# One matrix in place of two, and a new way for the routing data: a clustered attention and FFN kernel on one core

## The chip, the cores and the metric

The kernel runs on one core of a Trainium2 chip. The metric is device time in microseconds (us) of one execution of the program. TensorE is called PE here, VectorE DVE, ScalarE ACT, GpSimd POOL and SyncE SP, as the profile calls them; PEld is TensorE's loading of stationary operands. "DMA share" is the mean busy share of the core's 16 DMA engines, which by the profile's count can come out slightly above 1, "clock" the granted TensorE clock as a fraction of full speed.

A single core has no second core beside it to tell a disturbed run by. A run is called slow when it is over 1.5% above the fastest run of the same kernel. The times quoted for the experiments are medians of all runs, slow ones included; the ratios use fast runs alone.

## The reference, cut to what matters

There are 4 batches of 8 heads, 768 tokens and 64 dimensions. Every query and key is assigned to one of 16 clusters of its head, and attention is limited to pairs of the same cluster. The 3072 resulting rows of 512 go through a feed-forward network (FFN) whose only non-linearity is the product of two projections.

```python
q_assign = argmax(einsum(q_n, c_n));  k_assign = argmax(einsum(k_n, c_n))   # 16 clusters
mask   = q_assign[:, :, :, None] == k_assign[:, :, None, :]
scores = where(mask, scale * q @ k.T, -1e9)
attn   = softmax(scores) @ v                        # (4, 8, 768, 64)
x = attn.transpose(0, 2, 1, 3).reshape(3072, 512)
a = x @ w1                                          # (3072, 1024)
b = x @ w2
h = a * b @ w3                                      # w3 is (1024, 1024)
return h @ w_out                                    # w_out is (1024, 512)
```

Nothing stands between `@ w3` and `@ w_out`, so the two matrices can be multiplied beforehand.

## The kernel before

Each head passes four stages: load, prep, route, and scores with exp; the product with v follows one head later. Prep splits q and k into a bf16 part and a bf16 rest, side by side, and lets a transposing DMA turn them. ACT and DVE do the casts:

```python
stg = bstage.tile([P, 2, NCH, P], BF16, name="stg")
nc.scalar.copy(out=stg[:, 0, :, 0:D], in_=q32)
nc.vector.tensor_tensor(out=stg[:, 0, :, D:P], in0=q32, in1=stg[:, 0, :, 0:D], op=ALU.subtract)
# ... the same for k; v is cast on DVE ...
nc.sync.dma_start_transpose(out=xqk, in_=stg)
```

Route scores the clusters, builds a one-hot row per token, transposes it and writes it under the operand, in rows 64 to 79, so that the score matmul adds the mask by itself. It does so for q and for k, with six narrow transposes each:

```python
for which, sign in ((0, -1), (1, 1)):
    xt = xqk[:, which, :, :]
    prr = psum_f.tile([P, NCH, C, 2], F32, name="prr", tag="f")
    # ... six matmuls into prr; rsc = sum of its pairs; mx = maximum ...
    nc.vector.tensor_tensor(out=oh, in0=rsc, in1=mx..., op=ALU.is_ge)
    pso = psum_f.tile([P, NCH, P], BF16, name="pso", tag="f")
    for j in range(NCH):
        nc.tensor.transpose(out=pso[0:C, j, :], in_=oh[:, j, :], identity=ident)
    # ... DVE scales pso into xt[64 : 64 + C] ...
```

A score tile spans two PSUM banks (2 x 384 columns), and one exp reads it. The FFN of a batch runs in two blocks of 384 tokens, in units between the heads of the next batch (five units a head):

```python
def make_h(kc):                      # the product with w3
    def unit():
        ph = psum_f.tile([P, SH], F32, name="ph", tag="f")
        for jc in range(8):
            nc.tensor.matmul(ph, lhsT=w3b[:, jc, kc * P : (kc + 1) * P], rhs=abs_[:, jc, :],
                             start=(jc == 0), stop=(jc == 7))
        # ... hsb[:, kc] = ph, on ACT or DVE ...
def make_out(sub):                   # the product with w_out
    # ... po += hsb[:, kc, 128 tokens].T @ wob[:, kc]  for kc in 0..7 ...
```

The weights come as f32 through one staging buffer, each chunk cast on DVE, two chunks a head during the first 12 heads:

```python
ws = wstage.tile([P, DFF], F32, name="ws", tag="ws")      # the pool has one buffer
nc.scalar.dma_start(ws[:, 0:ncols], wsrc[:, cc, :])
nc.vector.tensor_copy(out=wdst[:, cc, :], in_=ws[:, 0:ncols])
```

The softmax here doesn't subtract the row's maximum and nothing guards it: scores larger than these inputs give would overflow.

Of the kernel before, what the change touches and what calls it, by code (L numbers as in the profile page):

```python
# [18 lines left out]
SH = 384  # L19
DFF = 1024  # L20
DM = 512
NTOK = B * S
MASKB = 256.0
SM_SCALE = 0.125
VCOL = D + 1
NG = B * H
FFN_UNITS_PER_HEAD = 5
# [3 lines left out]
def kernel(  # L31
# [12 lines left out]
    nc = tc.nc  # L44

    const = ctx.enter_context(tc.tile_pool(name="const", bufs=1))
    wstage = ctx.enter_context(tc.tile_pool(name="wstage", bufs=1))
    setup = ctx.enter_context(tc.tile_pool(name="setup", bufs=2))

    fstage = ctx.enter_context(tc.tile_pool(name="fstage", bufs=6))  # L50
    bstage = ctx.enter_context(tc.tile_pool(name="bstage", bufs=4))
    xtp = ctx.enter_context(tc.tile_pool(name="xtp", bufs=5))
    rtp = ctx.enter_context(tc.tile_pool(name="rtp", bufs=3))
    expp = ctx.enter_context(tc.tile_pool(name="expp", bufs=12))
    rcpp = ctx.enter_context(tc.tile_pool(name="rcpp", bufs=3))
    xtmp = ctx.enter_context(tc.tile_pool(name="xtmp", bufs=2))
    ffnp = ctx.enter_context(tc.tile_pool(name="ffnp", bufs=2))
    outp = ctx.enter_context(tc.tile_pool(name="outp", bufs=2))

    psum_sc = ctx.enter_context(tc.tile_pool(name="psum_sc", bufs=2, space=bass.MemoryType.PSUM))  # L60
    psum_av = ctx.enter_context(tc.tile_pool(name="psum_av", bufs=2, space=bass.MemoryType.PSUM))
    psum_f = ctx.enter_context(tc.tile_pool(name="psum_f", bufs=2, space=bass.MemoryType.PSUM))

    ident = const.tile([P, P], BF16, name="ident")
    make_identity(nc, ident)

    xT_all = const.tile([P, 4, NTOK], BF16, name="xT_all")

    cen = setup.tile([P, D], F32, name="cen")
    nc.sync.dma_start(cen, centroids.rearrange("h c d -> (h c) d"))  # L70
# [27 lines left out]
    cnt2 = const.tile([P, H, C, 2], BF16, name="cnt2")  # L98
    for which in range(2):
        pct = psum_f.tile([P, P], BF16, name="pct", tag="f")  # L100
        nc.tensor.transpose(out=pct, in_=cnsrc[:, which, :], identity=ident)
        nc.vector.tensor_copy(
            out=cnt2[:, :, :, which],
            in_=pct[:, :].rearrange("p (h c) -> p h c", c=C),
        )

    w1b = const.tile([P, 4, DFF], BF16, name="w1b")
    w2b = const.tile([P, 4, DFF], BF16, name="w2b")
    w3b = const.tile([P, 8, DFF], BF16, name="w3b")
    wob = const.tile([P, 8, DM], BF16, name="wob")  # L110

    wsrcs = []
    for wsrc, wdst, nchunks, ncols in (
        (moe_w1.rearrange("(fc p) j -> p fc j", p=P), w1b, 4, DFF),
        (moe_w2.rearrange("(fc p) j -> p fc j", p=P), w2b, 4, DFF),
        (moe_w3.rearrange("(jc p) kk -> p jc kk", p=P), w3b, 8, DFF),
        (moe_w_out.rearrange("(kc p) m -> p kc m", p=P), wob, 8, DM),
    ):
        for cc in range(nchunks):
            wsrcs.append((wsrc, wdst, cc, ncols))  # L120
    wcast_pending = list(wsrcs)

    def emit_weight_casts(n):
        for _ in range(n):
            if not wcast_pending:
                return
            wsrc, wdst, cc, ncols = wcast_pending.pop(0)
            ws = wstage.tile([P, DFF], F32, name="ws", tag="ws")
            nc.scalar.dma_start(ws[:, 0:ncols], wsrc[:, cc, :])
            nc.vector.tensor_copy(out=wdst[:, cc, :], in_=ws[:, 0:ncols])  # L130

    def block_units(t0: int):
        st = {}

        def make_ab(jc):
            def unit():
                if "asb" not in st:
                    st["asb"] = ffnp.tile([P, 8, SH], BF16, name="asb")
                    st["abs_"] = ffnp.tile([P, 8, SH], BF16, name="abs_")
                asb = st["asb"]  # L140
                abs_ = st["abs_"]
                pa = psum_f.tile([P, SH], F32, name="pa", tag="f")
                for fcc in range(4):
                    nc.tensor.matmul(  # L144
                        pa,
                        lhsT=w1b[:, fcc, jc * P : (jc + 1) * P],
                        rhs=xT_all[:, fcc, t0 : t0 + SH],
                        start=(fcc == 0),
                        stop=(fcc == 3),
                    )  # L150
                nc.scalar.copy(out=asb[:, jc, :], in_=pa)  # L151
                pb = psum_f.tile([P, SH], F32, name="pb", tag="f")
                for fcc in range(4):
                    nc.tensor.matmul(  # L154
                        pb,
                        lhsT=w2b[:, fcc, jc * P : (jc + 1) * P],
                        rhs=xT_all[:, fcc, t0 : t0 + SH],
                        start=(fcc == 0),
                        stop=(fcc == 3),
                    )  # L160
                nc.vector.tensor_tensor(out=abs_[:, jc, :], in0=pb, in1=asb[:, jc, :], op=ALU.mult)  # L161

            return unit

        def make_h(kc):
            def unit():
                if "hsb" not in st:
                    st["hsb"] = ffnp.tile([P, 8, SH], BF16, name="hsb")
                hsb = st["hsb"]
                abs_ = st["abs_"]  # L170
                ph = psum_f.tile([P, SH], F32, name="ph", tag="f")
                for jc in range(8):
                    nc.tensor.matmul(  # L173
                        ph,
                        lhsT=w3b[:, jc, kc * P : (kc + 1) * P],
                        rhs=abs_[:, jc, :],
                        start=(jc == 0),
                        stop=(jc == 7),
                    )
                if kc % 2 == 0:  # L180
                    nc.scalar.copy(out=hsb[:, kc, :], in_=ph)  # L181
                else:
                    nc.vector.tensor_copy(out=hsb[:, kc, :], in_=ph)  # L183

            return unit

        def make_out(sub):
            def unit():
                hsb = st["hsb"]
                po = psum_f.tile([P, 512], F32, name="po", tag="f")  # L190
                for kc in range(8):
                    nc.tensor.matmul(  # L192
                        po,
                        lhsT=hsb[:, kc, sub * P : (sub + 1) * P],
                        rhs=wob[:, kc, :],
                        start=(kc == 0),
                        stop=(kc == 7),
                    )
                osb = outp.tile([P, DM], F32, name="osb")
                nc.vector.tensor_copy(out=osb, in_=po)  # L200
                bb = t0 // S
                sb = (t0 % S) // P + sub
                out_perm = out.rearrange("(bb pp six) m -> bb six pp m", pp=P, six=NCH)
                nc.sync.dma_start(out_perm[bb, sb], osb)

            return unit

        units = [make_ab(jc) for jc in range(8)]
        units += [make_h(kc) for kc in range(8)]
        units += [make_out(sub) for sub in range(3)]  # L210
        return units

    def ffn_units(b: int):
        return block_units(b * S) + block_units(b * S + SH)

    state = {}

    def stage_load(g: int):
        b, h = g // H, g % H
        st = state.setdefault(g, {})  # L220
        q32 = fstage.tile([P, NCH, D], F32, name="q32")
        nc.sync.dma_start(q32, q[b, h].rearrange("(p j) d -> p j d", p=P))
        k32 = fstage.tile([P, NCH, D], F32, name="k32")
        nc.sync.dma_start(k32, k[b, h].rearrange("(p j) d -> p j d", p=P))
        v32 = fstage.tile([P, NCH, D], F32, name="v32")
        nc.sync.dma_start(v32, v[b, h].rearrange("(p j) d -> p j d", p=P))
        st["q32"], st["k32"], st["v32"] = q32, k32, v32

    def stage_prep(g: int):
        st = state[g]  # L230
        q32, k32, v32 = st["q32"], st["k32"], st["v32"]
        stg = bstage.tile([P, 2, NCH, P], BF16, name="stg")
        nc.scalar.copy(out=stg[:, 0, :, 0:D], in_=q32)
        nc.vector.tensor_tensor(
            out=stg[:, 0, :, D:P], in0=q32, in1=stg[:, 0, :, 0:D], op=ALU.subtract
        )
        nc.scalar.copy(out=stg[:, 1, :, 0:D], in_=k32)
        nc.vector.tensor_tensor(
            out=stg[:, 1, :, D:P], in0=k32, in1=stg[:, 1, :, 0:D], op=ALU.subtract
        )  # L240
        vb = xtp.tile([P, NCH, 72], BF16, name="vb")
        nc.vector.tensor_copy(out=vb[:, :, 0:D], in_=v32)
        nc.vector.memset(vb[:, :, D:VCOL], 1.0)
        xqk = xtp.tile([P, 2, NCH, P], BF16, name="xqk")
        nc.sync.dma_start_transpose(out=xqk, in_=stg)
        st["vb"], st["xqk"] = vb, xqk
# [110 lines left out]
    for i in range(5):  # L357
        stage_load(i)
# [57 lines left out]
```

## Time and profile before

The median of three runs was 491.62 us (488.81 to 492.89). I cut the profiled execution, 495 us long, into six stages. The start lasts until the first score matmul. Each batch's attention ends where its tokens are ready for the FFN. The tail is the rest. Batch 0 has no FFN of an earlier batch beside it; the tail has no attention.

| stage | length, us | what runs in it |
|---|---|---|
| start | 26.0 | loads, prep, first route |
| batch 0 | 99.0 | attention alone, weights arriving |
| batch 1 | 110.4 | attention + FFN of batch 0 |
| batch 2 | 104.8 | attention + FFN of batch 1 |
| batch 3 | 93.5 | attention + FFN of batch 2 |
| tail | 61.4 | FFN of batch 3 |

The first view is the page of the kernel before: the engine table (busy us, share of the span, instructions), then three rows of the strip of 40 slices. Each digit is the share in tenths: PE's busy share, its granted clock, the DMA share.

```profile
...
PE 398.6 (81%) x3514; PEld 237.7 (48%) x3522; DVE 238.3 (48%) x675; ACT 221.6 (45%) x355; POOL 0.7 (0%) x6
...
PE   0279555772877899997987999998999999699996
...
PEclk9999955565889899999799999999999999979999
DMA  8997989688878254237432332126111000310101
...
```

PE is busy in most of the span, but from the second to about the eighth slice the clock digits fall to 5 and PE's own digits are 5 to 8. The windows view of the same kernel, with one line for each stage, gives this in numbers. Its columns are named in its first line.

```profile
...
core 0: us, PE busy (x) PEld busy (x) DVE busy (x) ACT busy (x) POOL busy (x), PEclk, DMA share, GB/s
0.00:26.00 26.00, 3.08 (x32) 1.97 (x32) 14.72 (x52) 8.48 (x15) 0.70 (x6) 1.00 1.02 262
26.00:125.00 99.00, 62.73 (x615) 38.73 (x616) 47.00 (x144) 46.80 (x67) 0.00 (x0) 0.69 0.88 170
125.00:235.40 110.40, 96.45 (x878) 57.46 (x881) 63.07 (x177) 59.12 (x99) 0.00 (x0) 0.95 0.56 141
235.40:340.20 104.80, 94.45 (x879) 56.72 (x882) 54.58 (x156) 53.63 (x86) 0.00 (x0) 0.98 0.31 68
340.20:433.70 93.50, 85.30 (x811) 52.60 (x813) 41.42 (x116) 42.07 (x65) 0.00 (x0) 0.99 0.18 39
433.70:495.10 61.40, 56.55 (x302) 30.22 (x304) 17.54 (x30) 11.50 (x24) 0.00 (x0) 0.96 0.10 32
...
```

In batch 0 PE is busy for 62.7 us of 99, at a mean clock of 0.69, with a DMA share of 0.88. In batches 1 to 3 and the tail it is busy for 87 to 92%, at 0.95 to 0.99. The first part waits; the rest is bound by PE. The waits view of before names the waits (total us, times, longest us):

```profile
...
PE pso L276 <- DVE oh L268: 23.4, 16, 9.4
...
DVE w3b L130 <- DMA ws<-in_moe_w_dram: 19.2, 4, 6.5
...
PE prr L256 <- DMA xqk<-stg: 11.6, 2, 6.4
...
DVE w2b L130 <- DMA ws<-in_moe_w_dram: 8.4, 1, 8.4
...
```

A cast that waits for a weight chunk (19.2 and 8.4 us in two of the lines) holds the routing that follows it on DVE, and PE then waits for the one-hots (`oh`, 23.4 us). The three groups of the page that the change touches (busy us, mean ns of one, idle time before):

```profile
...
L312 ACT ACTIVATE ex<-sc 128x768 bf16<-128x768 f32 x192 | 147.6, 810 | 79.0 <-PE sc L304 58.2
L304 PE MATMUL sc<-xqk 80*128 80x384 bf16 x384 | 104.4, 362 | 15.9 <-ACT ex L312 11.5
...
L276 PE MATMUL pso<-ident,oh 128*16 128x128 bf16 x384 | 37.1, 241 | 23.9 <-DVE oh L268 23.4
...
```

The page's chain of waits, followed back from the last instruction, gives PE 54% of the span and the DMAs 23%, and names the product with w3 (`ph`) as the largest single part:

```profile
...
PE 54%; DMA 23%; DVE 10%; ACT 7%; issue 3%; SPq 2%; ACTq 0%; DVEq 0%
PE ph L173 13%; DMA xqk<-stg 11%; PE sc L304 9%; PE po L192 8%; PE pb L154 8%; PE pa L144 6%; DMA ws<-in_moe_w_dram 6%; PE pso L276 5%; ACT ex L312 5%; DMA xT_all<-xtm 2%; PE av L324 2%; DMA ws<-in_moe_w_out_dram 2%; PE prr L256 2%; SPq L35
...
```

### The profile page before, as it was taken

The page shows a single profiled execution, that of the slowest core. Times are in us where ns is not written, and L with a number is a line of the kernel's source. Part 1 is how long each engine was busy: PE and PEld are TensorE (multiplying, and loading weights), DVE is VectorE, ACT ScalarE, POOL GpSimd, SP SyncE. Part 2 cuts the span into 40 slices and gives each one's busy share as a digit, 9 for nine tenths or more (in the row PEclk, how much of TensorE's full clock was granted, in tenths as well). Part 3 has the DMA queues.
Part 4 walks back from the last instruction along what each step waited for, and adds up shares of the span by engine and source line. Part 5 has one row for each costly group of instructions (what it writes and reads, how often), then busy time and mean ns, then how long its engine had stood idle before and what let it go on. Part 6 is the DMA issues. An engine that isn't in the chain of part 4 may idle for free.

```text
span 495.1 us, 8793 instructions
## 1 busy us (share of the span) xinstructions
PE 398.6 (81%) x3514; PEld 237.7 (48%) x3522; DVE 238.3 (48%) x675; ACT 221.6 (45%) x355; POOL 0.7 (0%) x6
## 2 busy tenths in 40 slices
PE   0279555772877899997987999998999999699996
PEld 0146333441544456554554555555655666345453
DVE  5555454442486465545344655554545554222322
ACT  4157443433563456555533465546444645122120
POOL 0000000000000000000000000000000000000000
PEclk9999955565889899999799999999999999979999
DMA  8997989688878254237432332126111000310101
GB/s 290 233 320 195 88 194 92 188 104 192 229 193 218 84 129 102 74 77 163 107 49 49 71 89 50 33 75 119 33 33 47 19 1 1 97 32 1 64 1 64
DMA packets 84152, 51.98 MB, mean 105 GB/s; under 512 B 65680, under 2 KB 77968, under 8 KB 84112
## 3 DMA queue, kind: packets, MB, share of 16 engines
q1 hardware_dynamic: 80656, 40.94, 37.8%
q10 hardware_dynamic: 3456, 10.49, 8.3%
q8 instruction: 27, 0.44, 0.4%
q14 instruction: 13, 0.11, 0.1%
HBM read 29.39 MB, written 6.29 MB: 72 GB/s over the span
## 4 chain that ended last, share of the span: by engine, by line
PE 54%; DMA 23%; DVE 10%; ACT 7%; issue 3%; SPq 2%; ACTq 0%; DVEq 0%
PE ph L173 13%; DMA xqk<-stg 11%; PE sc L304 9%; PE po L192 8%; PE pb L154 8%; PE pa L144 6%; DMA ws<-in_moe_w_dram 6%; PE pso L276 5%; ACT ex L312 5%; DMA xT_all<-xtm 2%; PE av L324 2%; DMA ws<-in_moe_w_out_dram 2%; PE prr L256 2%; SPq L352 2%; DVE rsc L264 1%
## 5 line engine op out<-in xcount | busy, mean ns | idle before, releaser
L312 ACT ACTIVATE ex<-sc 128x768 bf16<-128x768 f32 x192 | 147.6, 810 | 79.0 <-PE sc L304 58.2
L304 PE MATMUL sc<-xqk 80*128 80x384 bf16 x384 | 104.4, 362 | 15.9 <-ACT ex L312 11.5
L173 PEld LDWEIGHTS <-w3b 128*128 128x128 bf16 x512 | 50.2, 99 | 41.0 <-issue 9.0
L324 PEld LDWEIGHTS <-ex 128*128 128x128 bf16 x1152 | 56.5, 103 | 27.6 <-issue 8.2
L144 PE MATMUL pa<-xT_all,w1b 128*128 128x384 bf16 x256 | 56.0, 344 | 16.9 <-DMA xT_all<-xtm 14.5
L151 ACT CAST asb<-pa 128x384 bf16<-128x384 f32 x64 | 30.6, 478 | 84.8 <-PE pa L144 84.8
L324 PE MATMUL av<-vb,ex 128*128 128x65 bf16 x1152 | 63.4, 202 | 5.4 <-DVE xtm L333 3.7
L154 PE MATMUL pb<-xT_all,w2b 128*128 128x384 bf16 x256 | 55.5, 341 | 1.4 <-DVE abs__1460 L161 0.3
L276 PE MATMUL pso<-ident,oh 128*16 128x128 bf16 x384 | 37.1, 241 | 23.9 <-DVE oh L268 23.4
L304 PEld LDWEIGHTS <-xqk 80*128 80x128 bf16 x384 | 31.8, 102 | 28.7 <-issue 16.3
L276 PEld LDWEIGHTS <-oh 128*16 128x16 bf16 x384 | 23.7, 97 | 40.2 <-DVE oh L268 34.6
L144 PEld LDWEIGHTS <-w1b 128*128 128x128 bf16 x256 | 24.8, 101 | 37.3 <-issue 17.3
L192 PE MATMUL po<-wob,hsb 128*128 128x512 bf16 x184 | 41.8, 379 | 0.4
L183 DVE CAST hsb<-ph 128x384 bf16<-128x384 f32 x32 | 17.8, 557 | 47.7 <-PE ph L173 47.7
L181 ACT CAST hsb<-ph 128x384 bf16<-128x384 f32 x32 | 15.3, 479 | 54.2 <-PE ph L173 54.2
L154 PEld LDWEIGHTS <-w2b 128*128 128x128 bf16 x256 | 25.5, 101 | 24.2 <-issue 9.6
L256 PE MATMUL prr<-cnt_141,xqk 128*128 128x32 bf16 x384 | 20.4, 181 | 11.6 <-DMA xqk<-stg 11.6
L192 PEld LDWEIGHTS <-hsb 128*128 128x128 bf16 x192 | 18.8, 98 | 21.7
L200 DVE COPY osb<-po 128x512 f32<-128x512 f32 x24 | 16.6, 691 | 21.7 <-PE po L192 21.7
L264 DVE TENSOR_REDUCE rsc<-prr 128x96 f32<-128x192 f32 x64 | 22.7, 354 | 8.9 <-PE prr L256 7.8
L278 DVE TENSOR_SCALAR xqk<-pso 16x768 bf16<-16x768 bf16 x32 | 17.6, 549 | 19.4 <-PE pso L276 18.9
L256 PEld LDWEIGHTS <-xqk 128*128 128x128 bf16 x384 | 16.7, 99 | 20.9 <-DMA xqk<-stg 11.9
(214 smaller groups left out, 310.8 us busy)
## 6 DMA issues: line engine op xcount, KB each, us to landing
ws<-in_moe_w_dram ACTq DMA_DIRECT2D x16, 512.0 KB, 4.1
out_dram<-osb SPq DMA_DIRECT2D x24, 256.0 KB, 2.0
ws<-in_moe_w_out_dram ACTq DMA_DIRECT2D x8, 256.0 KB, 3.1
xqk<-stg SPq DMA_TRANSPOSE x32, 4.6
xT_all<-xtm SPq DMA_TRANSPOSE x24, 2.5
q_152<-in_q_dram SPq DMA_DIRECT2D x1, 192.0 KB, 3.8
k_154<-in_k_dram SPq DMA_DIRECT2D x1, 192.0 KB, 3.8
v_156<-in_v_dram SPq DMA_DIRECT2D x1, 192.0 KB, 3.9
```

Source lines behind the costliest of these rows:

```text
L144: nc.tensor.matmul(pa, lhsT=w1b[:, fcc, jc * P : (jc + 1) * P], rhs=xT_all[:, fcc, t0 : t0 + SH], start=(fcc == 0), stop=(fcc == 3),)
L151: nc.scalar.copy(out=asb[:, jc, :], in_=pa)
L154: nc.tensor.matmul(pb, lhsT=w2b[:, fcc, jc * P : (jc + 1) * P], rhs=xT_all[:, fcc, t0 : t0 + SH], start=(fcc == 0), stop=(fcc == 3),)
L173: nc.tensor.matmul(ph, lhsT=w3b[:, jc, kc * P : (kc + 1) * P], rhs=abs_[:, jc, :], start=(jc == 0), stop=(jc == 7),)
L183: nc.vector.tensor_copy(out=hsb[:, kc, :], in_=ph)
L192: nc.tensor.matmul(po, lhsT=hsb[:, kc, sub * P : (sub + 1) * P], rhs=wob[:, kc, :], start=(kc == 0), stop=(kc == 7),)
L256: nc.tensor.matmul(prr[:, j, :, :], lhsT=xt[:, j, :], rhs=cnt2[:, h, :, :], start=True, stop=True,)
L264: nc.vector.tensor_reduce(out=rsc, in_=prr, axis=AX.X, op=ALU.add)
L276: nc.tensor.transpose(out=pso[0:C, j, :], in_=oh[:, j, :], identity=ident)
L304: nc.tensor.matmul(sc[:, sh, 0:SH], lhsT=xk[0:80, j, :], rhs=xq[0:80, 3 * sh : 3 * sh + 3, :], start=True, stop=True,)
L312: nc.scalar.activation(out=ex, in_=sc[:, :, 0:SH], func=ACT.Exp, scale=SM_SCALE)
L324: nc.tensor.matmul(av[:, sub, 0:VCOL], lhsT=exs[j][:, sh, sub * P : (sub + 1) * P], rhs=vb[:, j, 0:VCOL], start=(j == 0), stop=(j == NCH - 1),
```

## The change

Its intent is fourfold. The product `w3 @ w_out` is formed once on the chip, in units between the heads of batch 0, so the FFN has two steps instead of three. One-hots are built for q and k together and transposed four chunks at once (3 transposes in place of 12), and four small DMAs put them in place. The casts of q, k, v and the weights leave ACT and DVE (those inside the FFN stay): GpSimd casts q, k and v, and the weight loads, issued by GpSimd, cast on the way. Score tiles take one bank (512 columns, or 2 x 256), with three buffers. Besides, each pair of heads is transposed for the FFN on PE (`psx`) instead of by a DMA at the end of a batch, and the FFN works in blocks of 512 tokens. The core of the diff:

```diff
-            ws = wstage.tile([P, DFF], F32, name="ws", tag="ws")
-            nc.scalar.dma_start(ws[:, 0:ncols], wsrc[:, cc, :])
-            nc.vector.tensor_copy(out=wdst[:, cc, :], in_=ws[:, 0:ncols])
+            nc.gpsimd.dma_start(dst, src)            # f32 to bf16 on the way
 ...
+        def make_t(kc):                              # w3 transposed, 8 units
+            pt = psum_f.tile([P, 8, P], BF16, name="pt", tag="f")
+            for jc in range(8):
+                nc.tensor.transpose(out=pt[:, jc], in_=w3b[:, jc, kc * P : (kc + 1) * P], identity=ident)
+            nc.vector.tensor_copy(out=w3T[:, kc], in_=pt...)
+        def make_w(jc):                              # wc = w3 @ w_out, 8 units
+            pw = psum_f.tile([P, DM], F32, name="pw", tag="f")
+            for kc in range(8):
+                nc.tensor.matmul(pw, lhsT=w3T[:, kc, jc * P : (jc + 1) * P], rhs=wob[:, kc], ...)
+            nc.vector.tensor_copy(out=wc[:, jc], in_=pw)
 ...
-        def make_h(kc):  ...  (ph and hsb are gone)
-                        lhsT=hsb[:, kc, sub * P : (sub + 1) * P], rhs=wob[:, kc, :],
+                        po, lhsT=st["ab"][:, jc, sub * P : (sub + 1) * P], rhs=wc[:, jc],
 ...  prep
-        nc.scalar.copy(out=stg[:, 0, :, 0:D], in_=q32)
-        nc.vector.tensor_tensor(out=stg[:, 0, :, D:P], in0=q32, ..., op=ALU.subtract)   # and for k
+        nc.gpsimd.tensor_copy(out=stg[:, :, 0:D], in_=qk32)
+        nc.gpsimd.tensor_tensor(out=stg[:, :, D:P], in0=qk32, in1=stg[:, :, 0:D], op=ALU.subtract)
+        nc.gpsimd.tensor_copy(out=vb[:, :, 0:D], in_=x32[:, 2])
 ...  route
-            for j in range(NCH):                     # for q and for k
-                nc.tensor.transpose(out=pso[0:C, j, :], in_=oh[:, j, :], identity=ident)
+        for r in range(3):
+            nc.tensor.transpose(out=pso[:, r], in_=oh[:, r].rearrange("p a c -> p (a c)"), identity=ident)
+        nc.vector.tensor_scalar(out=ohT, in0=pso, scalar1=msc[:, 0:1], scalar2=msc[:, 1:2], ...)
+        for a in range(4):
+            nc.sync.dma_start(xqk[D : D + C, 3 * a : 3 * a + 3, :], ohT[32 * a : 32 * a + C])
 ...  scores
-            sc = psum_sc.tile([P, 2, 512], F32, name="sc")       # two banks, 2 buffers
-            nc.scalar.activation(out=ex, in_=sc[:, :, 0:SH], func=ACT.Exp, scale=SM_SCALE)
+                sc = psum_sc.tile([P, 512], F32, name="sc")      # one bank, 3 buffers
+                nc.scalar.activation(out=ex[:, i, 0:512], in_=sc, func=ACT.Exp, scale=SM_SCALE)
+            sc = psum_sc.tile([P, 2, 256], F32, name="sc")       # the last 256 columns of two chunks
+            nc.scalar.activation(out=ex[:, :, 512:S], in_=sc, func=ACT.Exp, scale=SM_SCALE)
 ...  main loop
+    pending = fold_units()
+        return 2 if g < H else 3                     # units a head: 2 in batch 0, then 3
```

## The prediction

> What bounds it now. By the page's engine table PE is busy 81% of 495 us, DVE 48%, ACT 45%. By stretches of the windows view: start 0 to 26 us (no scores yet); batch 0 attention alone, 26 to 121 us, PE busy 66% at a granted clock of 0.69 with DMA share 0.88; batches 1, 2, 3 with the FFN of the batch before, about 106, 105 and 95 us, PE 90 to 95% busy at 0.95 to 1.00; FFN tail 433 to 495 us. So batch 0 is bound by waits and a slow clock, the rest by PE. In batch 0 the waits view shows DVE held for weight chunks (27.7 us, longest 8.4 on w2b, while scores, casts and routing queue behind), PE for DMA xqk<-stg and for DVE oh. The Trainium skill, "TensorE: Matmul & The Clock Gate", section "What's actually happening", says an idle array falls to half clock; the trace agrees (0.50 from 60 to 100 us).
>
> PE work at full clock, from start-to-start spacing in the timeline: 384 columns 162 ns, 512 columns 216 ns (estimate by columns), a 128-column transpose about 56 ns, an av matmul about 35 ns. Before: scores 62, av 40, pa+pb 83, ph 83, po 41, pso 21, prr 12: about 343 us.
> After: ph vanishes (-83). The fold adds 64 transposes and 64 matmuls of 512 columns (+17). pso falls from 384 to 96 transposes (-16). Head-pair transposes psx add 96 (+5). Scores, av, pa, pb, po unchanged in columns. About 267 us: 76 less, nearly all on the critical path, since PE bounds batches 1 to 3 and the tail.
>
> Other engines. ACT: 192 exps of 768 columns (810 ns) become 288 of 512; from 810 and 478 ns at 768 and 384 columns I estimate 590 ns, so 147.6 to 170 us; the 64 casts of 0.5 us (-32) and hsb (-15) go. Total about 205: still hidden except in heads without FFN. DVE loses stg subtractions (35), v casts, weight casts (14), hsb (18), and halves its routing instruction count: 238 to about 145 us. GpSimd takes the casts: the skill's "GPSIMD Engine Reference", "Performance versus the Vector engine", gives 4497 ns for a 2048-element two-input op, so an estimate of 1.7 us for the 768-element subtraction, 3.5 to 4.5 us a head in all; no run shows it yet. Under a head's 8 us, so hidden, but it delays the first score (three serial preps). One-hot DMAs (4 of 12 KB a head) are hidden by routing two heads ahead. Batch 0 loses the DVE weight waits and gains fold work that helps the clock.
>
> Sum: start 22, batch 0 about 64 (8 us a head), batches 1 to 3 about 66, 84, 66 (12, 24, 12 FFN units), tail 48 (41.5 of PE, plus a transposition that no longer waits 5.3 us for DMA). Total 350 us, range 325 to 385. Faster 0.97, same 0.02, slower 0.01.
>
> Right if: no ph; PE busy near 290 to 310; exps 560 to 620 ns; tail about 47; batch 0's attention over by 80 to 95 us; DVE near 145; GpSimd 110 to 145. Wrong if: GpSimd takes over 7 us a head (or its SBUF traffic stretches DVE) and paces attention; fold transposes stall PE on the 4 MB of w3; SyncE's in-order queue holds loads behind one-hot DMAs; the single routing bank serializes route and psx; heads without FFN drop PE to half clock.

## The result, and the profile after

The kernel after took 348.0 us in the median (346.51 to 350.15, four runs), against 491.95 us for before in the same rounds (488.81 to 492.89, four runs). The ratio is 0.7096, with a 95% interval of 0.7051 to 0.7142. A ratio here is the mean time of one kernel's fast runs over the mean of the fast runs of before in the same rounds, so it is not quite the ratio of the medians quoted. The predicted total of 350 us was off by 2 us. The stages were not so good:

| stage | before | predicted after | after | error of the prediction's term |
|---|---|---|---|---|
| start | 26.0 | 22 | 36.5 | +14.5 |
| batch 0 | 99.0 | 64 | 70.3 | +6.3 |
| batch 1 | 110.4 | 66 | 63.7 | -2.3 |
| batch 2 | 104.8 | 84 | 79.6 | -4.4 |
| batch 3 | 93.5 | 66 | 53.7 | -12.3 |
| tail | 61.4 | 48 | 44.2 | -3.8 |
| sum | 495.1 | 350 | 348.0 | -2.0 |

The start and batch 0 took 20.8 us more than predicted, everything after them 22.8 us less. The right total is in part two errors that cancelled, which is luck. What follows asks where each came from.

The page after, with the same lines as above:

```profile
...
PE 287.2 (83%) x2818; PEld 171.6 (49%) x2818; DVE 159.4 (46%) x316; ACT 184.3 (53%) x351; POOL 102.3 (29%) x112
...
PE   0120748888999999879698989998999999799995
...
PEclk9999969899999999999899999999999999999999
DMA  7999799768798633697493474444502320001103
...
```

PE's busy time fell from 398.6 to 287.2 us, DVE's from 238.3 to 159.4, ACT's from 221.6 to 184.3, and POOL rose from 0.7 to 102.3. Of the hollow in the clock row one 6 is left, in the sixth slice. The windows view after, one line for each of the six stages (columns as in the windows of before; the last two are the DMA share and GB/s):

```profile
...
0.00:36.50 36.50, 5.09 (x62) 3.71 (x62) 12.28 (x43) 2.77 (x3) 19.15 (x27) 1.00 0.98 213
36.50:106.80 70.30, 60.29 (x662) 39.47 (x663) 36.38 (x69) 42.34 (x81) 32.07 (x34) 0.93 0.87 180
106.80:170.50 63.70, 56.43 (x631) 35.46 (x629) 31.64 (x62) 43.27 (x85) 23.88 (x25) 0.99 0.64 145
170.50:250.10 79.60, 74.14 (x716) 42.85 (x715) 41.65 (x73) 47.35 (x90) 26.16 (x26) 0.99 0.53 134
250.10:303.80 53.70, 51.44 (x569) 32.37 (x567) 23.61 (x51) 36.92 (x73) 1.01 (x2) 1.00 0.20 48
303.80:348.00 44.20, 39.82 (x183) 17.78 (x182) 13.82 (x20) 11.60 (x20) 0.00 (x0) 0.98 0.13 48
...
```

Batch 0 runs at a clock of 0.93, where it was 0.69. From batch 2 on PE is busy in 90 to 96% of each stage. The start and batch 0 stand at DMA shares of 0.98 and 0.87. The chain of waits after shows the same; the DMAs have 14% of it, and those named (`xqk<-stg`, the loads, `xqk<-ohT`) feed heads:

```profile
...
PE 65%; DMA 14%; DVE 11%; POOL 3%; SPq 2%; ACT 2%; issue 2%; DVEq 0%; POOLq 0%; ACTq 0%
PE po L232 12%; PE pb L220 12%; PE pa L212 12%; PE sc L299 9%; PE av L322 7%; DMA xqk<-stg 5%; PE sc L305 5%; PE pw L186 4%; DMA x_273<-in_v_dram 4%; PE pso L281 2%; DMA xqk<-ohT 2%; DMA x_113<-in_v_dram 2%; DVE rsc L269 2%; DVE oh_139 L273
...
```

The two groups of exps after, and then three lines of its waits view, which answer to those of before:

```profile
...
L302 ACT ACTIVATE ex<-sc 128x512 bf16<-128x512 f32 x192 | 107.2, 621 | 68.0 <-PE sc L299 67.6
...
L309 ACT ACTIVATE ex<-sc 128x512 bf16<-128x512 f32 x96 | 60.4, 630 | 11.6 <-PE sc L305 11.5
...
```

```profile
...
PE prr L267 <- DMA xqk<-stg: 17.2, 4, 6.7
...
PE sc L299 <- DMA xqk<-ohT: 10.2, 4, 3.7
...
PE pso L281 <- DVE oh_137 L273: 4.5, 5, 1.4
...
```

The exps take 621 and 630 ns. The busy times of the two groups add up to 167.6 us, but neighbouring exps overlap: asked for both together (the windows view of the tile `ex` on ACT), they occupy ACT for 147.2 us, no more than the 147.6 of before. Nothing waits for weights to be cast any more. The three buffers of the one-hots have a line each; the other two (3.4 and 3.3 us) make it 11.2 us, where before had 23.4. PE waits 17.2 us for transposed operands and 10.2 us for the DMAs of the one-hots, the longest 3.7 us.

The timeline after shows how the start went (start us, length us, engine, line, operation, count; SPq is SyncE issuing a DMA):

```profile
...
13.30 7.46 SPq L259 DMA_TRANSPOSE xqk<-stg  x2
...
16.04 2.17 POOL L108 DMA_DIRECT2D w3b<-in_moe_w_dram  x3
...
21.44 0.66 SPq L76 DMA_DIRECT2D x_273<-in_v_dram  x1
...
23.61 2.92 SPq L287 DMA_DIRECT2D xqk<-ohT  x4
...
33.62 3.34 SPq L287 DMA_DIRECT2D xqk<-ohT  x4
...
36.52 1.03 PE L299 MATMUL sc<-xqk 80*128 80x512 bf16 x2 [3.73 <-DMA xqk<-ohT]
...
```

The transposes of heads 1 and 2 were issued between 13.3 and 20.8 us; asked one by one, their issues took 1.28 and 4.64 us (the median of all 32 is 1.46), with a wait for the cast of head 2 between them. Three w3 loads were issued from 16 us, and two of w_out from 21.2 us, beside the k and v loads of the fifth head. Those two took 12.7 and 13.4 us to land, where most later ones took 2.5 to 4. The one-hot DMAs of head 0 were issued only at 23.6 us, those of head 1 at 33.6, and the first score began at 36.5. The Trainium skill, page "DMA: Bandwidth & Descriptors", section "Issuing engines are not separate DMA queues", says that DMAs of all issuers run on the same 16 engines and interleave. The trace agrees: these head loads, in flight together with weight loads and transposes, took three to five times as long.

### The profile page after: what moved, and what is told of

It is laid out like the page before. It is cut to its first block, busy times and chain, and to the rows that moved or that the text cites. A ratio compares the mean times of both kernels' runs of the same rounds, so it can differ in the third digit from the quotient of the medians.

```text
span 348.0 us, 7211 instructions
## 1 busy us (share of the span) xinstructions
PE 287.2 (83%) x2818; PEld 171.6 (49%) x2818; DVE 159.4 (46%) x316; ACT 184.3 (53%) x351; POOL 102.3 (29%) x112
## 4 chain that ended last, share of the span: by engine, by line
PE 65%; DMA 14%; DVE 11%; POOL 3%; SPq 2%; ACT 2%; issue 2%; DVEq 0%; POOLq 0%; ACTq 0%
PE po L232 12%; PE pb L220 12%; PE pa L212 12%; PE sc L299 9%; PE av L322 7%; DMA xqk<-stg 5%; PE sc L305 5%; PE pw L186 4%; DMA x_273<-in_v_dram 4%; PE pso L281 2%; DMA xqk<-ohT 2%; DMA x_113<-in_v_dram 2%; DVE rsc L269 2%; DVE oh_139 L273 2%; PE prr L267 2%
## 5 line engine op out<-in xcount | busy, mean ns | idle before, releaser
L302 ACT ACTIVATE ex<-sc 128x512 bf16<-128x512 f32 x192 | 107.2, 621 | 68.0 <-PE sc L299 67.6
L299 PE MATMUL sc<-xqk 80*128 80x512 bf16 x192 | 71.5, 396 | 11.6 <-DMA xqk<-ohT 10.2
L322 PEld LDWEIGHTS <-ex 128*128 128x128 bf16 x1152 | 63.2, 99 | 22.3 <-issue 5.6
L309 ACT ACTIVATE ex<-sc 128x512 bf16<-128x512 f32 x96 | 60.4, 630 | 11.6 <-PE sc L305 11.5
L217 ACT CAST asb<-pa 128x512 bf16<-128x512 f32 x48 | 27.8, 586 | 47.0 <-PE pa L212 46.9
L212 PE MATMUL pa<-xT_all,w1b 128*128 128x512 bf16 x192 | 52.0, 381 | 0.6 <-DVE xT_all L344 0.6
L220 PE MATMUL pb<-xT_all,w2b 128*128 128x512 bf16 x192 | 52.0, 380 | 0.2 <-ACT asb L217 0.2
L224 DVE TENSOR_TENSOR ab<-pb,asb 128x512 bf16<-128x512 f32 x48 | 33.2, 691 | 41.0 <-PE pb L220 35.6
L232 PE MATMUL po<-wc,ab 128*128 128x512 bf16 x192 | 43.1, 379 | 0.0
L305 PE MATMUL sc<-xqk 80*128 80x256 bf16 x192 | 38.8, 280 | 0.0
L269 DVE TENSOR_REDUCE rsc<-prr 128x192 f32<-128x384 f32 x32 | 17.6, 551 | 33.8 <-PE prr L267 33.8
L267 PE MATMUL prr<-cnt_189,xqk 128*128 128x32 bf16 x384 | 15.4, 178 | 17.7 <-DMA xqk<-stg 17.2
L232 PEld LDWEIGHTS <-ab 128*128 128x128 bf16 x192 | 18.5, 98 | 21.7
L299 PEld LDWEIGHTS <-xqk 80*128 80x128 bf16 x192 | 17.4, 100 | 12.7 <-DMA xqk<-ohT 11.7
```

The costliest lines, as they stand in the source:

```text
L212: nc.tensor.matmul(pa, lhsT=w1b[:, fc, js], rhs=xT_all[:, fc, t0 : t0 + TB], start=(fc == 0), stop=(fc == 3),)
L217: nc.scalar.copy(out=asb, in_=pa)
L220: nc.tensor.matmul(pb, lhsT=w2b[:, fc, js], rhs=xT_all[:, fc, t0 : t0 + TB], start=(fc == 0), stop=(fc == 3),)
L224: nc.vector.tensor_tensor(out=st["ab"][:, jc], in0=pb, in1=asb, op=ALU.mult)
L232: nc.tensor.matmul(po, lhsT=st["ab"][:, jc, sub * P : (sub + 1) * P], rhs=wc[:, jc], start=(jc == 0), stop=(jc == 7),)
L267: nc.tensor.matmul(prr[:, j], lhsT=xqk[:, j, :], rhs=cnt2[:, h], start=True, stop=True)
```

## The experiments

The theory of work, W, says that the gain is above all TensorE work taken from stages that TensorE bounds, which is the fold. The rival says that it comes from batch 0's flow of data: the weight casts off DVE, the casts on GpSimd, the wide one-hots, the one-bank tiles. A second question came with the result: why the start and batch 0 took longer than predicted, whether by the order in which DMAs are issued, or by their sum. Twelve kernels ran, all with correct results. Each ratio is to before. Stage lengths were cut in the same way throughout.

### 1. After, without the fold

```diff
-    pending = fold_units()
+    pending = []
+        def make_h(kc):  ...  ph, lhsT=w3b[:, jc, ...], rhs=st["ab"][:, jc]  ...
-                        po, lhsT=st["ab"][:, jc, sub * P : (sub + 1) * P], rhs=wc[:, jc],
+                        po, lhsT=st["h"][:, jc, sub * P : (sub + 1) * P], rhs=wob[:, jc],
-    return 2 if g < H else 3
+    return 0 if g < H else 5
```

> The changed kernel with the two last products separate again (h = ab @ w3, then h @ w_out), all else as changed. Theory W (the gain is mostly TensorE work taken away, and TensorE bounds the FFN stretches): 66 us of full-clock TensorE work come back, so 405 to 420 us, about +60 to +72, with the FFN tail 20 us longer and attention of batches 1 to 3 about 10 to 18 us longer each, and batch 0 a few us shorter. Rival R (most of the gain is waits removed; TensorE has slack): under 375 us.

It took 421.6 us, ratio 0.8568 (0.8489 to 0.8648): 73.6 us more than after. PE was busy for 357.0 us. Its windows for batches 1, 2, 3 and the tail (columns as before):

```profile
...
99.50:178.00 78.50, 71.78 (x679) 41.55 (x678) 33.38 (x67) 43.77 (x85) 31.56 (x32) 0.93 0.63 150
178.00:279.90 101.90, 101.42 (x840) 56.31 (x840) 40.84 (x80) 51.06 (x98) 26.18 (x26) 1.00 0.41 105
279.90:347.60 67.70, 65.20 (x633) 38.56 (x631) 26.35 (x54) 39.43 (x77) 1.01 (x2) 1.00 0.15 38
347.60:419.50 71.90, 67.44 (x311) 30.31 (x310) 19.41 (x29) 16.28 (x28) 0.00 (x0) 0.99 0.08 30
...
```

Against after, these four stages took 14.8, 22.3, 14.0 and 27.7 us more; batch 0, which no longer held the fold's own work, was 8 us shorter. The tail's 27.7 us agree with the work in it: two blocks of 64 matmuls of 512 columns, at 216 ns from start to start, are 27.6 us. My expectation of about 20 us for the tail was too small. This supports W: undoing the fold alone gives back half of the 144 us.

### 2. Before, with the fold alone

```diff
+        if b == 0:
+            return a0 + a1 + fold_units() + o0 + o1      # the fold in batch 1
-        units += [make_h(kc) for kc in range(8)]
-                        lhsT=hsb[:, kc, sub * P : (sub + 1) * P], rhs=wob[:, kc, :],
+                        lhsT=st["abs_"][:, kc, sub * P : (sub + 1) * P], rhs=wc[:, kc, :],
```

(`asb` also became a small tile per unit, so that everything fits in SBUF.)

> The kernel before with only the fold added (done in batch 1, after the first FFN inputs) and the separate product with w3 dropped. Theory W: 66 us of TensorE work less, nearly all in TensorE-bound stretches: 425 to 440 us, tail 21 us shorter. Rival R: above 455 us, because waits fill the gap.

It took 436.77 us, ratio 0.8899 (0.884 to 0.8958): 54.7 us less than before, within what was expected. The windows of its batch 1 and tail:

```profile
...
117.00:235.90 118.90, 99.78 (x909) 58.62 (x910) 69.43 (x187) 56.76 (x93) 0.00 (x0) 0.91 0.54 130
...
396.00:436.00 40.00, 35.00 (x176) 17.50 (x176) 13.07 (x22) 7.65 (x16) 0.00 (x0) 0.96 0.16 50
...
```

The tail fell from 61.4 to 40 us. Batch 1 rose from 110.4 to 118.9 us, as it now holds the fold, whose weights come last through the one staging buffer. So the fold is worth 55 us from this side and 74 from the other. A likely reason for the difference, which no run isolates: after can do the fold in batch 0, where PE has idle time, because its weights arrive earlier; before can't.

### 3. Before, with the weight casts moved from DVE to GpSimd

```diff
-            nc.vector.tensor_copy(out=wdst[:, cc, :], in_=ws[:, 0:ncols])
+            nc.gpsimd.tensor_copy(out=wdst[:, cc, :], in_=ws[:, 0:ncols])
```

> The kernel before, with only the weight casts moved from VectorE to GpSimd. Theory H (in batch 0 VectorE, held in order for slow weight loads, held up attention): about 20 to 28 us less, 464 to 472 us, batch 0 attention shorter than 80 us. Rival (batch 0 is paced by DMA itself): within 5 us of before.

It took 473.75 us, ratio 0.966 (0.9586 to 0.9734): 17.7 us less, below the 20 to 28 expected. The window of batch 0 (cut at 26 us as in before; the first score came at 27.8):

```profile
...
26.00:100.00 74.00, 57.16 (x608) 35.37 (x609) 43.40 (x135) 46.28 (x67) 12.12 (x12) 0.82 0.82 216
```

Batch 0 fell from 99 to 74 us and its clock rose from 0.69 to 0.82. The prediction had counted 27.7 us of DVE waits for weight chunks in this stage; taking them off DVE won 25 of them there, and the clock came with it. The next stage didn't give them back: batch 1, cut as in before where the next `pa` waits for its tokens (in the timeline of PE at 210.58 us, on the DMA `xT_all<-xtm`), lasted from 100.1 to 210.6 us, so 110.5 us as against 110.4. The whole span fell by 23.0 us (495.1 to 472.1), the medians by 17.7; the profiled execution of before was longer than its median run.

### 4. After, with the weight loads and the fold later in program order

```diff
-    emit_wloads(4)                     # before the first route
-            emit_wloads(2)
+            if g >= 1:
+                emit_wloads(2)
-    return 2 if g < H else 3
+    if g < 4:
+        return 0
+    return 4 if g < H else 3
```

> The changed kernel with the first weight loads moved behind the first heads' loads and the fold done in heads 4 to 7, four units a head. Theory S (the first score comes at 36.5 us instead of the predicted 22 because 6 MB of weights share the DMA engines with the first heads' loads and transposes): first score at 20 to 26 us, total 334 to 340 us. Rival (SyncE's in-order queue or the serial GpSimd preps set the start): first score stays above 32 us, total 345 to 350 us.

It took 350.51 us, ratio 0.7125 (0.7053 to 0.7196), and tells nothing. The loads have nothing to wait for, and the instruction scheduler put them early again: the trace shows the first w3 load issued at 1.28 us, two more at 18.7 and the rest by 25.9. The first score came at 38.4 us. The edit didn't make the change that it was meant to make.

### 5. The same with a true dependency

Each weight load now waits for a one-column copy by GpSimd from a head's one-hots into the weight tile.

```diff
+            nc.gpsimd.tensor_copy(out=dst[:, 0, 0:1], in_=gate[:, 0, 0:1])
             nc.gpsimd.dma_start(dst, src)
+    emit_wloads(2, state[1]["ohT"])
+                emit_wloads(1, state[g + ROUTE_AHEAD]["ohT"])
```

> The weight loads now truly held: a one-column GpSimd copy from a routed head's one-hots into the weight tile, ahead of each load, keeps the load until that head is routed (two loads after head 1, one more per head after that); fold in heads 4 to 7. In the run before this one the scheduler had moved the loads back to the front, so the weights were on the DMA engines as early as ever. Theory S (weights crowd out the first heads' loads and transposes): first score at 20 to 27 us, total 336 to 343 us. Rival Q (SyncE issues one-hot DMAs behind transposes in order, weights or not): first score still above 32 us, total unchanged at 346 to 352.

It took 344.87 us, ratio 0.698 (0.6903 to 0.7056), an interval that touches that of after; the profiled run (347.17) was slow. The windows of its start and batch 0:

```profile
...
0.00:20.10 20.10, 3.02 (x44) 2.04 (x44) 14.74 (x41) 2.77 (x3) 13.29 (x20) 1.00 0.85 209
20.10:104.20 84.10, 65.36 (x673) 42.67 (x677) 35.64 (x72) 43.52 (x81) 36.76 (x48) 0.90 1.01 180
...
```

The start fell from 36.5 to 20.1 us, about the 22 that I had predicted. So the weight loads in the first 20 us made the start late, but not alone: experiment 7 leaves them early, takes away the one-hot DMAs, and begins at 22.3 us. But batch 0 rose from 70.3 to 84.1 us, with the DMA engines busy throughout (1.01), and ended at 104.2 us instead of 106.8. Bringing the first score forward by 16 us brought the end of the batch forward by 2.6. So when the weights are loaded hardly matters for that end; that points to the sum of the DMAs (0.85 x 20.1 + 1.01 x 84.1 = 102 us of DMA work by then, 97 in after). The two fast runs took 341.59 and 342.57 us, so a fast execution may have ended the batch some us earlier than this profile.

### 6. After, with the head casts on ACT and DVE again

```diff
-        nc.gpsimd.tensor_copy(out=stg[:, :, 0:D], in_=qk32)
-        nc.gpsimd.tensor_tensor(out=stg[:, :, D:P], in0=qk32, in1=stg[:, :, 0:D], op=ALU.subtract)
+        nc.scalar.copy(out=stg[:, :, 0:D], in_=qk32)
+        nc.vector.tensor_tensor(out=stg[:, :, D:P], in0=qk32, in1=stg[:, :, 0:D], op=ALU.subtract)
-        nc.gpsimd.tensor_copy(out=vb[:, :, 0:D], in_=x32[:, 2])
+        nc.vector.tensor_copy(out=vb[:, :, 0:D], in_=x32[:, 2])
```

> The changed kernel with the q, k, v casts back on ScalarE and VectorE instead of GpSimd. Theory (casts are off the critical path on any engine in the FFN stretches; about 32 us more on ScalarE, 38 on VectorE, both under 70% busy): 345 to 356 us. Rival (moving casts to GpSimd was a real part of the gain, because in-order ScalarE and VectorE hold casts behind exps): 360 us or more.

It took 367.21 us, ratio 0.7488 (0.7426 to 0.7549): 19 us more than after. The casts on GpSimd are worth something, but this run mixes two causes. With GpSimd free, all weight loads were issued within 12 us, and the first score came at 46.7 us, 10.2 later than after. The rest of the loss is in batch 2 (91.3 us against 79.6), where ACT waits for a free `stg` behind its transposing DMA (37.6 us in all, longest 19.4) and DVE waits for ACT (40.2 us); the exps and the FFN's instructions follow those on the same two engines. The run also showed what one instruction costs when GpSimd is quiet. This is the group that builds the one-hots (busy us, mean ns):

```profile
...
L273 DVE TENSOR_TENSOR oh<-rsc,mx 128x192 bf16<-128x192 f32 x32 | 11.4, 356 | 0.9
...
```

In after the same instruction has a mean of 793 ns. Two lines of after's timelines, of DVE and then of POOL, show why (start us, length us):

```profile
...
204.81 1.63 DVE L273 TENSOR_TENSOR oh_139<-rsc,mx 128x192 bf16<-128x192 f32 x1
...
```

```profile
...
204.59 1.64 POOL L255 TENSOR_TENSOR stg<-x_3474,stg 128x768 bf16<-128x768 f32 x1
...
```

DVE's instruction started at 204.81 and ended at 206.44; GpSimd's subtraction started at 204.59 and ended at 206.23. DVE's took 1.63 us instead of 0.36, and was done 0.2 us after GpSimd's. The Trainium skill, "GPSIMD Engine Reference", section "Specifications", says that GpSimd shares its SBUF interface with VectorE and contends with instructions that have two SBUF inputs. The trace agrees (this one has two), and gives the size: of the 32 one-hot instructions of after, all 15 that started beside a running subtraction ended 0.21 or 0.22 us after it, and the 12 that met nothing on GpSimd took 0.36. Over 32 heads the excess is 32 x (0.793 - 0.356) = 14.0 us of DVE time. What it costs in total time was not tested by itself.

### 7. After, with twelve narrow transposes and no one-hot DMA

```diff
-        for r in range(3):
-            nc.tensor.transpose(out=pso[:, r], in_=oh[:, r]..., identity=ident)
-        for a in range(4):
-            nc.sync.dma_start(xqk[D : D + C, 3 * a : 3 * a + 3, :], ohT[32 * a : 32 * a + C])
+        for which in range(2):
+            for j in range(NCH):
+                nc.tensor.transpose(out=pso[0:C, j, :], in_=oh[:, which * NCH + j, :], identity=ident)
+            nc.vector.tensor_scalar(out=xqk[D : D + C, which * NCH : (which + 1) * NCH, :], in0=pso[0:C], ...)
```

> The changed kernel with the one-hots transposed a chunk at a time (12 narrow transposes a head, VectorE writes them straight into the operand tile, no DMA). Theory W: 288 more transposes of 56 ns, 16 us more TensorE work, and 20 us more VectorE, minus the DMA hop: 356 to 368 us in all, but the first score earlier than 36 us. Rival (the wide transposes bought little, since the four DMAs a head cost SyncE time and latency): 348 us or less.

It took 355.15 us, ratio 0.7256 (0.7193 to 0.7318): 7 us more than after, at the low end of what was expected, with 20.2 us more of PE busy time. The first score came at 22.3 us, 14.2 earlier than after, without the one-hot DMAs. And yet batch 0 ended at 108.6 us, in a profile of a fast run. This is the second run in which an early start is lost by the end of batch 0.

### 8. After, with two-bank score tiles

```diff
-                sc = psum_sc.tile([P, 512], F32, name="sc")          # 3 buffers, psum_f 3
+                sc = psum_sc.tile([P, 2, 512], F32, name="sc")       # 2 buffers, psum_f 2
+                nc.scalar.activation(out=ex[:, i]..., in_=sc[:, :, 0:384], func=ACT.Exp, scale=SM_SCALE)
```

> The changed kernel with two-bank score tiles as before the change: six exps of 768 columns a head instead of nine of 512, two tiles of two banks, and two instead of three banks for the FFN. Theory (ScalarE is hidden behind TensorE): ScalarE busy falls by about 20 us, total within 344 to 356 us. Rival A (ScalarE paces the heads without FFN): 335 to 343 us. Rival B (one-bank tiles were needed for overlap): 358 us or more.

It took 352.64 us, ratio 0.7178 (0.711 to 0.7247), 4.6 us more than after, but the intervals overlap. The exps occupied ACT for 142.0 us (811 ns each) instead of 147.2, and ACT was busy for 179.4 us instead of 184.3. That is 5 us less and not the 20 expected, since neighbouring exps overlap (see the result). So the run hardly tests whether ACT is a limit, and which of the two tilings is better can't be told from it.

### 9 to 11. After, with batch 0's operands transposed on PE

If the sum of the DMAs bounds batch 0, taking DMA work away must end it earlier. For the first eight heads, PE transposes the operands (12 transposes a head and two copies by DVE):

```diff
+PE_T = 8
-        nc.sync.dma_start_transpose(out=xqk, in_=stg)
+        if g >= PE_T:
+            nc.sync.dma_start_transpose(out=xqk, in_=stg)
+        if g < PE_T:                                  # at the start of the route
+            for a in range(2):
+                pxt = psum_f.tile([P, NCH, P], BF16, name="pxt", tag="f")
+                for j in range(NCH):
+                    nc.tensor.transpose(out=pxt[:, j], in_=stg[:, a * NCH + j, :], identity=ident)
+                nc.vector.tensor_copy(out=xqk[:, a * NCH : (a + 1) * NCH, :], in_=pxt)
```

> The changed kernel with the operand transposes of the first eight heads done on TensorE (12 transposes a head into PSUM, two VectorE copies) instead of by DMA. Gating the weights brought the first score from 36.5 to 20.7 us and yet the last attention of batch 0 ended only 2.5 us sooner, with a DMA share near 1. Theory D (the first 106 us are set by the sum of DMA work: weights, loads, transposes): taking 8 DMA transposes of about 3.5 us away ends batch 0 at 78 to 92 us and the total at 322 to 338 us, though TensorE work grows by 5 us. Rival P (a head's dependent steps or TensorE set batch 0): batch 0 still ends at 103 to 110, total 346 to 355 us.

It took 333.56 us (330.7 to 335.67), ratio 0.6762 (0.6699 to 0.6826). Its interval lies wholly below that of after, and 0.6762 / 0.7096 = 0.953, so it is 4.7% faster than after. It is the fastest kernel. The profiled run (335.67) was slow. The windows of its start and batch 0:

```profile
...
0.00:26.40 26.40, 8.39 (x93) 6.82 (x94) 14.53 (x46) 2.77 (x3) 20.28 (x29) 1.00 0.90 231
26.40:91.30 64.90, 62.22 (x733) 42.10 (x730) 39.02 (x82) 41.38 (x81) 33.23 (x34) 0.97 0.79 182
...
```

Batch 0 ended at 91.3 us instead of 106.8 (a slow run would rather end it later; experiment 12 gives a fast one). The work of the DMA engines up to that point (share times length) was 0.98 x 36.5 + 0.87 x 70.3 = 96.9 us in after and 0.90 x 26.4 + 0.79 x 64.9 = 75.0 us here. Eight transposes thus took about 21.9 us of all 16 engines, an estimate of 2.7 us for each. The first score, too, came 10 us earlier. PE was now busy for 62.2 of the 64.9 us, so in this kernel PE is what bounds batch 0. The edit takes away three things at once: the DMA work of the transposes, each head's wait for its transpose to land (3.7 to 16.1 us in after), and their place in SyncE's queue. No run separates them.

Two sister kernels added the gate of experiment 5 to the weight loads. The first has the same eight heads on PE, the second eleven (`PE_T = 11`):

```diff
+            nc.gpsimd.tensor_copy(out=dst[:, 0, 0:1], in_=gate[:, 0, 0:1])      # both, as in experiment 5
-PE_T = 8
+PE_T = 11                                                                   # the second only
```

> The same, with the weight loads also held until heads are routed (as in the gated run). Theory D with S: the start of 20 us is now worth something, because DMA no longer sets the end of batch 0; 5 to 12 us less than the run without the gate, 316 to 330 us. Rival: the gate delays the weights that the fold needs, and it is equal or slower.

> The same with the gate, and the first eleven heads' transposes on TensorE. If DMA still bounds batch 0 with eight (three more heads' transposes are issued ahead within it), 3 to 8 us less again; if not, 1 to 3 us more for the added TensorE work in batch 1.

They took 338.58 us (ratio 0.6854, 0.6781 to 0.6926) and 338.06 us (0.6816, 0.6744 to 0.6888); both profiled runs were slow. Batch 0 ended at 99.1 and 94.8 us in those profiles, later than without the gate (91.3, also of a run marked slow). The intervals overlap with the ungated kernel's, so that the gate hurts is likely and not shown, and the two sisters can't be told from each other. The gate brought no gain; that it delays the fold once the transposes are gone is a likely reason, not a tested one.

### 12. All 32 heads transposed on PE

```diff
-PE_T = 8
+PE_T = 32
```

> As the run with TensorE transposes for the first eight heads, but for all 32 heads, weights not gated. Batch 0 should end where it did with eight (86 to 92 us). Theory D with W (DMA bounds only batch 0, TensorE bounds the rest): 24 heads more at 12 transposes of 56 ns are 16 us of TensorE work added where TensorE is the bound, so 343 to 352 us, 10 to 18 us above the eight-head run. Rival (DMA transposes cost time everywhere through late operands): 334 us or less.

It took 337.48 us (336.33 to 338.56), ratio 0.6894 (0.6775 to 0.7013). That lies between what the theory (343 to 352) and the rival (334 at most) expected. PE was busy for 306.2 us, 19 more than in after. Its profile is of a fast run, and it confirms the end of batch 0, here at 92.8 us:

```profile
...
0.00:26.20 26.20, 8.30 (x90) 6.73 (x91) 14.45 (x46) 2.77 (x3) 20.16 (x29) 1.00 0.91 232
26.20:92.80 66.60, 63.13 (x768) 43.30 (x769) 41.93 (x88) 41.12 (x81) 28.76 (x30) 0.97 0.60 148
...
```

Why the added PE work in batches 1 to 3 cost little, I can only argue: in this kernel the one-hot instruction has a mean of 442 ns, and its part in the chain of waits from 107 to 300 us is 2.2 us, against 13.1 in after and 12.6 in the kernel with eight heads. The casts no longer wait for a transposing DMA, so they fell elsewhere in time. No run tested that alone.

### What the twelve say together

| undone or added | us, against after | us, against before |
|---|---|---|
| fold | +73.6 without it | -54.7 with it alone |
| head casts on GpSimd | +19.2 without them (mixed with a later start) | not run |
| weight casts off DVE | not run | -17.7 with it alone |
| wide one-hots by DMA | +7.2 without them | not run |
| one-bank score tiles | +4.6 without them (unclear) | not run |
| operands of batch 0 transposed on PE | -14.4 with it | not run |

The differences are of medians from different calls. The parts don't add up to 144 us from either side. Probably they help one another: weights that come early and uncast let the fold sit in batch 0's idle PE time. And no run undid the transposition of the head pairs on PE (`psx`), the FFN blocks of 512 tokens or, in after, the loads that cast, so what these are worth stays open.

For the end of batch 0, five kernels with transposing DMAs (after, and experiments 4, 5, 7 and 8) have their first scores at 20 to 38 us and end the batch at 104 to 109 us, whatever the start. The four with PE transposes end it at 91 to 99. That is what the theory of the DMA sum asks for, and the times of the weight loads and the one-hot DMAs are ruled out as the main cause; that it is the sum, and not each head's wait for its transpose, is argued. It isn't the only term: without the fold (experiment 1), with the same weights loaded, the batch ended at 99.5 us, so the fold's 17 us of PE work cost some 7 of them there. By then the DMA work was 0.96 x 37.6 + 0.79 x 61.9 = 85.0 us, 12 less than in after; so these sums are estimates, and not the same in every kernel. In after's chain of waits, too, the transposing DMAs stand only in the first part of batch 0; from 80 us on it is PE work, the fold's `pw` above all (37%). The slow first score of experiment 6 also moved the end, to 116.2 us.

## Why the prediction was right, and where only its sum was

- **No `ph`, and the fold as the main gain: right.** There is no `ph` in the profile. PE busy came out at 287.2 us, just under the predicted 290 to 310. Two runs, from both sides, give the fold 74 and 55 us of the 144.
- **Tail about 47: nearly right.** It is 44.2 us. The terms were 41.5 us of PE and 6.5 of waits; beyond that PE work it took 2.7.
- **Batch 3 at 66 us: mis-sized by 12.3.** By the prediction's own figures, attention without the fold is (62 + 40 + 5 + 12 + 5) / 4 = 31.0 us of PE a batch and one FFN block is (83 + 41) / 6 = 20.7, so 51.7 us of work; I added 14.3 for waits. It took 53.7 us, so 2.0 beyond that work. In batches 1 and 2 I had added 14.3 and 11.6 and they needed 12.0 and 7.2. I carried over the looseness of before, whose batch 3 had 8.2 us without PE busy. That these waits came from what the change removed fits the profile (waits for one-hots fell from 23.4 to 11.2 us, those for weight casts are gone), but no run isolates it.
- **Start at 22 us: wrong by 14.5.** The prediction said that "three serial preps" delay the first score, but took no account of 4 MB of w3 and the one-hot DMAs on the same DMA engines. Experiment 5, with the weights held back, began at 20.1 us, experiment 7, without the one-hot DMAs, at 22.3.
- **Batch 0 over by 80 to 95 us: wrong, it was 106.8.** Of the 20.8 us that it was late, 14.5 are the start and 6.3 the stage itself. The step "One-hot DMAs (4 of 12 KB a head) are hidden by routing two heads ahead" failed as such: PE waited 10.2 us for them, 3.7 just before the first score, 1.9 in batch 0 and 4.6 in batch 1. But it is not what made the batch late, since experiment 7 did without them and ended it at 108.6 us. In batch 0 PE waited longer for transposed operands (5.4 us), and the predicted 64 us had left the DMA work out. The windows of before had shown a DMA share of 0.88 in batch 0. I read the waits there as waits for DVE, and took them off (experiment 3 confirms 25 us in that stage), but did not add up the DMA work that would then be the next limit.
- **Clock in batch 0: higher, as said, but not by the fold.** The Trainium skill, "TensorE: Matmul & The Clock Gate", section "What's actually happening", was the source for half clock in an idle array; with PE busy in 60.3 of 70.3 us the clock was 0.93. The prediction had put this down in part to "fold work that helps the clock"; experiment 1, without the fold, had 0.94 there.
- **Exps 560 to 620 ns and ACT about 205 us: the first just missed, the second too high.** They took 621 and 630 ns; ACT was busy for 184.3. The step that failed is count times mean time ("147.6 to 170 us"): exps overlap, and their ACT time stayed at 147.2. That ACT is hidden is argued from the stages (in batch 3 PE was busy for 51.4 us and ACT for 36.9); experiment 8 took only 5 us of ACT time away.
- **DVE about 145 us: 14 too low.** The measured 159.4 contains 14.0 us of stretched one-hot instructions. "Or its SBUF traffic stretches DVE" stood among the risks, and it happened.
- **GpSimd 3.5 to 4.5 us a head: a little too high.** It took 0.82 + 1.64 + 0.51 = 3.0 us, and 102.3 us in all where 110 to 145 was said. The 1.7 us estimated for the subtraction, from the skill's "GPSIMD Engine Reference", section "Performance versus the Vector engine", were 1.64.
- **Of the other risks**, the SyncE queue came true in the start. The transposition of w3 did stall PE, for 5.7 us in two waits before the first score. The single routing bank and a half clock in heads without FFN did not show, but for one slice at 0.6.

What stays open: whether batch 0 is held by the sum of the DMAs or by each head's wait for its transpose, what the collisions between GpSimd and DVE cost in total time, whether two-bank tiles are worse, and why exactly the kernel with all heads on PE lost so little.

## What to carry to other kernels

Make two sums for each stage, TensorE work and DMA work (share times length), before and after the change: when the change removes a wait, the larger of the two is a candidate for what comes next. Where the DMA sum was the larger (experiments 5 and 7), a start that came 14 to 16 us earlier moved the end of the stage by 2.6 us at most. An allowance for waits shouldn't be carried over from a kernel whose cause of waiting the change removes. When an experiment is to move something in time, give it a true dependency and look in the trace whether it moved, since the scheduler may put it back.

## What the Trainium skill lacked or had wrong

- "VectorE: DVE Perf Modes", section "The three transpose paths", says that the transposing DMA runs at about 90% of DMA bandwidth. Here the transposition of 128 x 1536 bf16 (393 KB) took about 2.7 us of all 16 engines (an estimate from two DMA sums), some 144 GB/s; a second estimate, from the share of SyncE's queue over the whole of after (0.470 x 348.0 us) and of the kernel with none left (0.252 x 335.3 us), gives 2.5 us. The window from 0 to 26 us of before moved 262 GB/s at a share of 1.02, so by that measure it ran at little over half.
- "TensorE: Matmul & The Clock Gate", section "PE-mode transpose", says about 390 ns in isolation, 275 ns in context, and that full clock doesn't engage. In the kernels with PE transposes twelve of them took 0.83 us at 219 ns each, so (0.83 - 0.22) / 11 = 55 ns from start to start, with the granted clock at 1.00. They ran among other matmuls; whether transposes alone would raise the clock isn't shown.
- No page read here says how long SyncE needs to issue small DMAs when the engines are full: 0.54 us each in the median of 128, and 3.3 us for one of those of the first 45 us.
